# Third block of the experts' first layer by seven products of 256 tokens, with its operand sums moved and the schedule's table renewed

## The chip, the core and the metric

The kernel runs on one core of a Trainium2 chip. A core has five engines that run side by side, each through its own list of instructions in a fixed order: TensorE (PE) for matmuls, VectorE (DVE), ScalarE (ACT) and GpSimd (POOL) for elementwise work, and SyncE (SP), which here starts DMAs. Matmul results land in PSUM, eight banks of 128 rows by 512 floats; everything else lies in SBUF. The metric is the device time of one execution in microseconds (us): 1002.8 us before, the median of three runs (1002.5 to 1004.2).

## The reference, cut to what matters

Three stages follow one another: attention in which a query sees only keys of the same hash bucket, a gated layer, and four experts whose outputs are weighted and added.

```
bits   = (q @ proj > 0), (k @ proj > 0);  bucket = sum bits * 2**i      # 2 x 8 heads, 768 tokens, 64 wide
scores = where(bucket_q == bucket_k, scale * q @ k.T, -1e9);  attn = softmax(scores) @ v
x      = attn, heads side by side                                       # 1536 tokens x 512
x      = ((x @ w1) * (x @ w2)) @ w3 @ w_out                             # 1024 wide inside, 512 out
p      = domain_probs / (sum + 1e-9)
out    = sum over e of p[:, e] * (relu(x @ W1[e]) @ W2[e])              # 4 experts, 512 -> 1024 -> 512
```

## The kernel before

All products are made at nearly fp32 accuracy: every operand is split into a rounded part and the rest ("hi" by a copy to fp32r, `hi_of` L154 on ACT or `pool_hi` L160; "lo" by a subtraction, `lo_of` L157 on DVE or `pool_lo` L163), and a product is three matmuls, hi x hi, hi x lo and lo x hi (`T3`). A full matmul is 128 x 128 weights against 512 columns. The 1536 tokens go in three blocks of 512.

*Attention.* 48 units (`unit`, L405), each 256 queries of one head: scores into PSUM (`s_ps`), a minimum with its row value on DVE (L426), the exponential on ACT (L429), a normalisation on POOL or ACT, twelve transposes on PE, their split by ACT (L466) and DVE (L468), and twelve 256-column matmuls with v (`pv_ps`). `head` (L312) loads and splits q and k and copies pieces between tiles by DMA on SP's queue; v comes by L362 in rows of 64 floats. Beside it the first gate weights are loaded (L196) and split (`conv64`, L180), and a quarter of block 0's gate layer is multiplied as a filler.

*Gate.* Both products of the gate for all blocks, then w3 times w_out (`W`), then for each block eight steps `H` (24 half-size groups, twelve matmuls each) that multiply the gate's result, split just before by ACT and DVE into one of two `hl` tiles, into four banks: `o_ps` for blocks 0 and 2, `u_ps` for block 1.

*Experts.* An expert's hidden layer goes in four quarters of 256 columns. Blocks 0 and 1 are multiplied together by seven products M1 to M7 in place of eight (a Strassen scheme in Winograd's form: sums of quadrants of x on one side, of W1 on the other), six full matmuls each, in the order 4, 3, 1, 2, 5, 7, 6. ACT copies M4 and M3 out of PSUM; DVE adds the others to running sums (`mix`, L933 with L881): two sums from each of M1, M2 and M5, one from M7 and M6. A bank of the four `u_ps` comes free when its last reader is done. Block 2's part of the quarter follows as two plain groups `U` (L974) of twelve full matmuls, and then `put_down` multiplies block 0's part of the quarter by W2 (24 full matmuls). After four quarters come blocks 1 and 2 against W2.

The operand sums of x for M1, M3, M4, M6 and M7 are made once, in the third block's H steps: L859 on POOL, ten of 128 x 512, each followed by a hi on ACT and a lo on DVE into `xh` and `slot` tiles. W1 is split by POOL (`conv_full`, L730, whole tile: L161 then L164), and its five sums per quarter by DVE (L750) with a hi on ACT (L155) and a lo on DVE into `slotl` and `zs`.

*What sets the order.* The program lists operations with an engine, an assumed duration, what they need, and a priority; `emit_all` (L244) plays them once through at build time and so fixes every engine's order. The priority of attention's operations is shifted by the table `RANK` (L25); operations of the later stages take their place from a running clock.

## Time and profile before

| | us |
|---|---|
| three runs, median | 1002.8 (1002.5 to 1004.2) |
| the profiled execution | 1005.64 |
| its span on the core | 1003.9 |
| PE busy, DVE busy, ACT busy, POOL busy | 977.6, 662.0, 432.4, 313.4 |
| attention, until PE is in the gate's late part | about 274 |

The profile was taken in one execution of 1005.64 us; about 1.7 us of it lie around the span. TensorE had its full clock (the granted clock is 1.00 in every stretch). Matmuls overlap one another, so PE's busy share says little about how full it is; how many matmuls began in a stretch says more. The chain of waits, followed back from the last instruction, lies on PE for 73% and on DVE for 18%.

### The profile page before, as it was taken

How to read it: one execution, taken by the hardware profiler on the slowest of the kernel's cores; microseconds unless marked ns; L12 is line 12 of the kernel's file. 1: busy time of each engine (PE TensorE's matmuls, PEld its weight loads, DVE VectorE, ACT ScalarE, POOL GpSimd, SP SyncE). 2: the span in 40 equal slices, each digit the busy share in tenths (PEclk: the TensorE clock that was granted, in tenths of full speed). 3: DMA queues.
4: the chain of work that ended last, by engine and by line, in shares of the span. 5: the costliest groups of instructions: out<-in, count | busy, mean ns of one | idle time of the engine just before them, and what ended most of it. 6: DMA issues, size and time to landing. Idle time of an engine off the chain costs nothing.

```text
span 1003.9 us, 13346 instructions
## 1 busy us (share of the span) xinstructions
PE 977.6 (97%) x4939; PEld 822.7 (82%) x4939; DVE 662.0 (66%) x1194; ACT 432.4 (43%) x779; POOL 313.4 (31%) x297
## 2 busy tenths in 40 slices
PE   7899999999999999999799999999999999999998
PEld 6788888988788888888588888888888888888886
DVE  6799999998499984954965444554445544455343
ACT  5789999988533332434422221222212222122121
POOL 6777788764000000041641204212042120421000
PEclk9999999999999999999999999999999999999999
DMA  5853554321033331320210101101011010100012
GB/s 159 192 130 79 130 122 107 93 61 42 1 105 121 124 113 39 109 84 1 63 43 26 38 1 57 49 26 39 0 59 48 27 37 1 57 28 21 1 50 77
DMA packets 51137, 64.13 MB, mean 64 GB/s; under 512 B 17688, under 2 KB 34072, under 8 KB 51072
## 3 DMA queue, kind: packets, MB, share of 16 engines
q1 hardware_dynamic: 50928, 63.27, 22.1%
q8 instruction: 39, 0.64, 0.3%
q14 instruction: 26, 0.21, 0.1%
q10 hardware_dynamic: 144, 0.01, 0.0%
HBM read 47.22 MB, written 3.15 MB: 50 GB/s over the span
## 4 chain that ended last, share of the span: by engine, by line
PE 73%; DVE 18%; ACT 3%; issue 2%; DMA 2%; POOL 1%; SPq 0%; DVEq 0%; ACTq 0%
PE u_ps L149 50%; PE o_ps L149 19%; DVE et L468 5%; DVE e L426 5%; PE t_ps L149 2%; DMA r<-in_qk 1%; ACT e L429 1%; DVE xa L487 1%; PE pv_ps L149 1%; PE t_ps L460 1%; PE s_ps L149 1%; ACT et L466 1%; DVE hl L158 1%; DVE xh L158 1%; DVE hl L876 1%
## 5 line engine op out<-in xcount | busy, mean ns | idle before, releaser
L149 PE MATMUL u_ps<-xh,slot 128*128 128x512 f32 x768 | 179.9, 389 | 1.2 <-DVE xh L158 1.2
L149 PE MATMUL o_ps<-slotl,hl 128*128 128x512 f32 x768 | 178.2, 390 | 0.4 <-DVE hl L876 0.2
L149 PEld LDWEIGHTS u_ps<-xh,slot 128*128 128x128 f32 x768 | 144.1, 188 | 31.5 <-DVE xh L158 1.6
L149 PEld LDWEIGHTS o_ps<-slotl,hl 128*128 128x128 f32 x768 | 143.9, 188 | 31.5 <-DVE hl L876 1.7
L881 DVE TENSOR_TENSOR m<-m,u_ps 128x512 f32<-128x512 f32 x96 | 62.9, 683 | 138.4 <-ACT m L155 114.7
L161 POOL TENSOR_SCALAR slot<-wraw 128x1024 fp32r<-128x1024 f32 x16 | 17.3, 1080 | 384.6 <-DVE slotl L158 184.1
L149 PE MATMUL u_ps<-xh,slotl 128*128 128x512 f32 x480 | 111.6, 389 | 0.0
L149 PEld LDWEIGHTS u_ps<-xh,slotl 128*128 128x128 f32 x480 | 90.1, 188 | 18.7
L468 DVE TENSOR_TENSOR et<-t_ps,et 128x512 fp32r<-128x512 f32 x144 | 96.5, 680 | 5.3 <-ACT et L466 4.7
L429 ACT ACTIVATE e<-e,sm 128x768 f32<-128x768 f32 x96 | 89.6, 934 | 12.3 <-DVE e L426 10.8
L426 DVE TENSOR_SCALAR_CACHE_REDUCE e<-s_ps 128x768 f32<-128x768 f32 x96 | 90.3, 945 | 4.3 <-PE t_ps L460 3.1
L149 PE MATMUL pv_ps<-et,vv 128*128 128x256 f32 x576 | 91.8, 295 | 0.9 <-DVE xa L487 0.7
L460 PE MATMUL t_ps<-ident,e 128*128 128x128 f32 x576 | 85.6, 276 | 6.7 <-DVE et L468 4.8
L466 ACT ACTIVATE et<-t_ps 128x512 fp32r<-128x512 f32 x144 | 83.0, 593 | 12.5 <-PE t_ps L460 5.8
L149 PE MATMUL u_ps<-slotl,hl 128*128 128x512 f32 x384 | 87.7, 389 | 0.0
L149 PEld LDWEIGHTS u_ps<-slotl,hl 128*128 128x128 f32 x384 | 72.1, 188 | 15.0
L460 PEld LDWEIGHTS t_ps<-ident,e 128*128 128x128 f32 x576 | 65.2, 140 | 16.9 <-DVE et L468 7.9
L149 PEld LDWEIGHTS pv_ps<-et,vv 128*128 128x128 f32 x576 | 75.0, 190 | 3.4 <-DVE xa L487 2.8
L439 POOL TENSOR_SCALAR e<-e,sm 128x768 f32<-128x768 f32 x72 | 65.7, 921 | 18.4 <-DVE sm L444 15.0
L155 ACT ACTIVATE m<-u_ps 128x512 f32<-128x512 f32 x32 | 19.1, 598 | 107.0 <-PE u_ps L149 107.0
L873 ACT ACTIVATE hl<-m 128x512 fp32r<-128x512 f32 x32 | 20.3, 633 | 92.3 <-DVE m L881 92.3
L876 DVE SCALAR_TENSOR_TENSOR hl<-gl,hl 128x512 fp32r<-128x512 f32 x32 | 23.8, 742 | 54.3 <-ACT hl L995 46.2
(142 smaller groups left out, 1534.9 us busy)
## 6 DMA issues: line engine op xcount, KB each, us to landing
wraw<-in_e SPq DMA_DIRECT2D x64, 256.0 KB
wraw<-in_w SPq DMA_DIRECT2D x16, 512.0 KB
wraw<-in_w3T SPq DMA_DIRECT2D x16, 512.0 KB
r<-in_qk SPq DMA_DIRECT2D x15, 384.0 KB
wraw<-in_w_out SPq DMA_DIRECT2D x8, 512.0 KB
rv<-in_v SPq DMA_DIRECT2D x16, 192.0 KB
out<-xa SPq DMA_DIRECT2D x12, 256.0 KB
ka<-hh SPq DMA_DIRECT2D x15, 192.0 KB
```

What stands on the lines that cost most here:

```text
L149: nc.tensor.matmul(out=o, lhsT=l, rhs=r, start=start, stop=stop)
L155: nc.scalar.activation(out=dst, in_=ps, func=AF.Copy)
L158: nc.vector.tensor_tensor(out=dst, in0=ps, in1=f(hi), op=ALU.subtract)
L426: op(("mx", u, t), "DVE", 873, lambda ps=ps, m=m, e=e: nc.vector.tensor_scalar(out=e, in0=ps[:, 0:S], scalar1=THR, scalar2=None, op0=ALU.m ...
L429: op(("ex", u, t), "ACT", 921, lambda e=e, m=m, rs=rs: nc.scalar.activation(out=e, in_=e, func=AF.Exp, scale=-1.0, bias=m, accum_out=rs), ...
L439: return "POOL", 872, lambda: nc.gpsimd.tensor_scalar(out=e, in0=e, scalar1=r[:, t:t + 1], scalar2=1.0, op0=ALU.mult, op1=ALU.mult)
L460: nc.tensor.transpose(out=ps[:, k, t * 128:(t + 1) * 128], in_=e_t[2 * (u % ER) + t][:, kt * 128:(kt + 1) * 128], identity=ident)
L466: op(("hi", n), "ACT", 480, lambda ps=ps, et=et: nc.scalar.activation(out=et[:, 0], in_=ps, func=AF.Copy), [("T", u, j), ("pv", n - NET)], Tj)
L468: op(("lo", n), "DVE", 602, lambda ps=ps, et=et: nc.vector.tensor_tensor(out=et[:, 1], in0=ps, in1=f(et[:, 0]), op=ALU.subtract), [("hi", ...
L873: op(key, "ACT", 480, lambda: nc.scalar.activation(out=hl_t[n % 2][:, 0], in_=m_t[m], func=AF.Relu), after, clock[0])
L876: op(key, "DVE", 602, lambda: nc.vector.scalar_tensor_tensor(out=hl_t[n % 2][:, 1], in0=src(), scalar=0.0, in1=f(hl_t[n % 2][:, 0]), op0=A ...
L881: nc.vector.tensor_tensor(out=out, in0=a, in1=b, op=o)
```

## The change

*Products.* Block 2 no longer has the plain groups `U`. Its 512 tokens are taken as two halves of 256, and seven products N1 to N7 (same scheme, same W1 sums, order 4, 3, 1, 2, 5, 7, 6) of six matmuls of 256 columns each stand in their place; the results are joined by `mix` on 256 columns straight into the tiles that are kept. `mul` and `mix` get a width and an operand set. The W1 tile itself is now needed only in two of its four pieces, and POOL splits these two alone, in four instructions of 128 x 256. The W1 sums of the next quarter may overwrite the old ones once the N products, not the M products, have read them.

*Operands.* Block 2's result is copied out of `o_ps` (ACT), five sums of halves are made on DVE (`ys`), and seven operands are split (`yi` on ACT, `yd` on DVE). The sums for the M products move from POOL to DVE, one source in PSUM; M4's are made one block earlier.

*Loads and the first head.* v lies in memory so that a row of 1.5 KB per partition holds a head. The first head's query bits are written in two pieces (256 and 512 columns), and the next head's lo part is queued behind them on DVE. The load of head 2 waits for more of head 0's operations. The assumed durations and the table are new, so that attention's order is another on every engine.

```diff
 RANK = {
...
-    "ex0": -95.56,
-    "ex1": -444.49,
+    "ex0": 16.57,
+    "ex1": -26.35,
...
-            op(("ld", hh), "SP", 1130, lambda: load(slice(0, 2 * D)), [("l", hh - RR)] if hh >= RR else [],
+            op(("ld", hh), "SP", 2000, lambda: load(slice(0, 2 * D)), [(x, hh - RR) for x in (("l", "k1", "k2", "k3", "dq") if hh == RR else ("l",))],
                -1e9 + 1e7 * hh if first else T - 8000)
             if first:
...
-                op(("l", hh), "DVE", 870, lambda: scaled_lo(nc.vector), [("h", hh)], T, g)
+                op(("l", hh), "DVE", 1000, lambda: scaled_lo(nc.vector), [("h", hh), ("mq", 0)], T, g)
...
-        op(("lv", hh), "SP", 600, lambda: nc.sync.dma_start(out=rv, in_=v[b, h].rearrange("(k p) d -> p k d", p=128)),
+        op(("lv", hh), "SP", 1000, lambda: nc.sync.dma_start(out=rv, in_=v[b, h].rearrange("p (k d) -> p k d", k=NK)),
...
-        op(("mk", 0), "DVE", 865, lambda: is_pos(kb[k], ps, k), [("bm", -1)], T, "b0")
-        op(("mq", 0), "DVE", 865, lambda: is_pos(lo[64:64 + PC], ps, q), [("mk", 0)], T, "b0")
-        keys[("sf", n)] = keys[("mq", 0)]
+        op(("mk", 0), "DVE", 930, lambda: is_pos(kb[k], ps, k), [("bm", -1)], T, "b0")
+        for i, (key, c) in enumerate(((("mq", 0), slice(0, 256)), (("sf", n), slice(256, S)))):
+            op(key, "DVE", (330, 600)[i], lambda c=c: is_pos(lo[64:64 + PC, c], ps, q, c), [("mk", 0)], T + i, "b0")
...
+            rq = r.rearrange("p (j k f c) -> p j f k c", j=2, k=2, f=2)
+            for i in range(2):
+                key = ("dd" if i else "dc", name)
+                op(("dh", name, i), "POOL", 310, lambda i=i: pool_hi(a_at(fp, i)[:, 0], rq[:, i, i]), got + after, T)
+                op(key, "POOL", 640, lambda i=i: pool_lo(a_at(fp, i)[:, 1], rq[:, i, i], a_at(fp, i)[:, 0]), [("dh", name, i)], T)
...
+            for m, o, a, b in ((4, ALU.subtract, (1, 0), (0, 0)), (3, ALU.subtract, (0, 1), (1, 1)), (1, ALU.add, (0, 0), (1, 1)),
+                               (2, None, (0, 0), None), (5, None, (1, 1), None), (7, ALU.add, (1, 0), (1, 1)), (6, ALU.add, (0, 0), (0, 1))):
...
+                op(("yi", m), "ACT", 520, lambda m=m, src=src: hi_of(by(m)[:, 0], src()), ready, T + 9 * Q)
+                op(("yd", m), "DVE", 602, lambda m=m, src=src: lo_of(by(m)[:, 1], src(), by(m)[:, 0]), [("yi", m)], T + 9 * Q)
...
+        for m, a, (b, c), o in sums:
             for k in range(2):
-                op(("xs", m, k), "POOL", 1225, lambda m=m, a=a, b=b, o=o, k=k: nc.gpsimd.tensor_tensor(
-                    out=xs(m)[:, k], in0=G[a[0]][:, a[1] + k], in1=G[b[0]][:, b[1] + k], op=o),
...
+                op(("xs", m, k), "DVE", 602, lambda m=m, a=a, b=b, c=c, o=o, k=k, hb=hb: nc.vector.tensor_tensor(
+                    out=xs(m, k), in0=hb[a + k], in1=G[b][:, c + k], op=o),
...
-            for ff in (2 * fp, 2 * fp + 1):
-                n, free_ = take_u()
...
-                op(("U", e, 2, ff), "PE", 12 * 227, go, free_ + have_u + x_in + [("hl", 2, d) for d in range(KM)], clock[0])
...
+            for m, dst, lhs in ((4, C21, lambda fp=fp: a_at(fp, 1)), (3, C12, lambda fp=fp: a_at(fp, 0))):
+                n, got = mul(m, lhs, have_u, "N", by, W)
+                op(("uf", n), "ACT", 270, lambda n=n, dst=dst: hi_of(dst(), u_ps[n % 4][:, 0:256]), got + old + y_in, clock[0])
+                keys[key(f"y{m}")] = keys[("uf", n)]
+            n, got = mul(1, lambda: z(0), have_z, "N", by, W)
+            mix("ya1", C11, C21, n, ALU.add, got + old + y_in + [key("y4")], W)
+            mix("yb1", C22, C12, n, ALU.add, got + old + y_in + [key("y3"), key("ya1")], W)
```

PE in the second quarter of the first expert, from M6 (operands `slot` and `zs`) on. Before: M6, the two plain groups of block 2, and the start of the product with W2.

```order
L149 MATMUL u_ps_3041<-slot_63,zs 128x512 x6
L149 MATMUL u_ps_3038<-xh_3020,slot_65 128x512 x12
L149 MATMUL u_ps_3039<-xh_3020,slot_65 128x512 x12
L149 MATMUL o_ps_3042<-slotl_3022,hl_3029 128x512 x3
L149 MATMUL o_ps_3043<-slotl_3022,hl_3029 128x512 x3
```

The two plain groups are 24 matmuls of 512 columns.

Now, at the same place:

```order
L149 MATMUL u_ps_3040<-slot_63,zs 128x512 x6
L149 MATMUL u_ps_3041<-xh_3021,slot_64 128x256 x6
L149 MATMUL u_ps_3042<-xh_3021,slot_64 128x256 x6
L149 MATMUL u_ps_3043<-xh_3021,slotl_3022 128x256 x6
L149 MATMUL u_ps_3040<-xh_3021,slotl_3022 128x256 x6
L149 MATMUL u_ps_3041<-slot_65,slotl_3022 128x256 x6
L149 MATMUL u_ps_3042<-y,slotl_3022 128x256 x6
L149 MATMUL u_ps_3043<-slot_65,zs 128x256 x6
L149 MATMUL o_ps_3044<-slotl_3023,hl_3030 128x512 x3
```

The seven rows of 128x256 are N4, N3, N1, N2, N5, N7 and N6 in the place of the two rows of 128x512 x12; N6 now reads `zs` seven products later than M6 did.

PE in the first quarter of the first expert, behind the third block's last H step, from M6 on. Before:

```order
L149 MATMUL u_ps_3040<-slot_63,zs 128x512 x6
L149 MATMUL u_ps_3041<-xh_3020,slot_64 128x512 x12
L149 MATMUL u_ps_3038<-xh_3020,slot_64 128x512 x12
L149 MATMUL o_ps_3042<-slotl_3026,hl_3029 128x512 x3
L149 MATMUL o_ps_3043<-slotl_3026,hl_3029 128x512 x3
L149 MATMUL o_ps_3044<-slotl_3026,hl_3029 128x512 x3
```

The order is that of the other quarters.

Now, at the same place, down to N7:

```order
L149 MATMUL u_ps_3042<-slot_63,zs 128x512 x6
L149 MATMUL u_ps_3043<-xh_3021,slot_64 128x256 x6
L149 MATMUL o_ps_3044<-slotl_3027,hl_3030 128x512 x3
L149 MATMUL o_ps_3045<-slotl_3027,hl_3030 128x512 x3
L149 MATMUL o_ps_3046<-slotl_3027,hl_3030 128x512 x3
L149 MATMUL o_ps_3047<-slotl_3027,hl_3030 128x512 x3
L149 MATMUL u_ps_3043<-slot_65,slotl_3022 128x256 x6
L149 MATMUL u_ps_3042<-xh_3021,slotl_3022 128x256 x6
L149 MATMUL u_ps_3040<-xh_3021,slot_64 128x256 x6
L149 MATMUL u_ps_3041<-xh_3021,slotl_3022 128x256 x6
L149 MATMUL u_ps_3040<-y,slotl_3022 128x256 x6
```

Here the N products are taken apart: N4 alone, then half of the product with W2 (the four rows of `o_ps`), then N5, N2, N3, N1 and N7; behind the rows shown come the other half (`hl_3031`), N6 and M4 of the second quarter. `u_ps_3042` and `u_ps_3040` are the banks of M6 and M5.

DVE behind the third block's last H step. Before: the last W1 sums (`slotl`, `zs`), block 2's four lo parts out of `o_ps`, and the first mixes (`m`, `g`) of the first quarter.

```order
L158 TENSOR_TENSOR zs<-zf,zs 128x256
L158 TENSOR_TENSOR xh_3020<-o_ps_3042,xh_3020 128x512
L158 TENSOR_TENSOR xh_3020<-o_ps_3043,xh_3020 128x512
L158 TENSOR_TENSOR xh_3020<-o_ps_3044,xh_3020 128x512
L158 TENSOR_TENSOR xh_3020<-o_ps_3045,xh_3020 128x512
L881 TENSOR_TENSOR m_3034<-m_3032,u_ps_3040 128x512
L881 TENSOR_TENSOR m_3035<-m_3033,u_ps_3040 128x512
L881 TENSOR_TENSOR m_3032<-m_3032,u_ps_3041 128x512
L881 TENSOR_TENSOR m_3035<-m_3035,u_ps_3041 128x512
L881 TENSOR_TENSOR g_67<-m_3033,u_ps_3038 128x512
```

Only four lo parts (sources in PSUM) stand between the W1 sums and the first mixes.

Now: sums of halves (`gl_3028`), lo parts of the N operands (`xh_3021`, `slot_65`, `y`) and mixes in turn. First piece:

```order
L158 TENSOR_TENSOR zs<-zf,zs 128x256
L875 TENSOR_TENSOR gl_3028<-gl_3029 128x512 x2
L924 TENSOR_TENSOR m_3035<-m_3033,u_ps_3042 128x512
L158 TENSOR_TENSOR xh_3021<-gl_3028,xh_3021 128x2x256
L924 TENSOR_TENSOR m_3036<-m_3034,u_ps_3042 128x512
L924 TENSOR_TENSOR m_3033<-m_3033,u_ps_3043 128x512
L158 TENSOR_TENSOR xh_3021<-gl_3028,xh_3021 128x2x256
L924 TENSOR_TENSOR m_3036<-m_3036,u_ps_3043 128x512
L919 SCALAR_TENSOR_TENSOR hl_3030<-m_3033,hl_3030 128x512
```

The first two sums of halves and two lo parts have come ahead of mixes.

and the piece behind it:

```order
L875 TENSOR_TENSOR gl_3028<-gl_3029 128x512
L158 TENSOR_TENSOR xh_3021<-gl_3029,xh_3021 128x2x256
L158 TENSOR_TENSOR slot_65<-gl_3029,slot_65 128x512
L158 TENSOR_TENSOR xh_3021<-gl_3028,xh_3021 128x2x256
L875 TENSOR_TENSOR gl_3028<-gl_3029 128x512 x2
L158 TENSOR_TENSOR y<-gl_3028,y 128x512
L158 TENSOR_TENSOR slot_65<-gl_3028,slot_65 128x512
L924 TENSOR_TENSOR g_67<-m_3034,u_ps_3040 128x512
L924 TENSOR_TENSOR g_67<-m_3036,u_ps_3042 128x512
L924 TENSOR_TENSOR m_3035<-m_3035,u_ps_3040 128x512
```

From the first sum of halves to the last row shown, which is the last reader of M5's bank, stand 20 instructions; before there were four lo parts and then the mixes.

SP at the start of attention. Before, a load of gate weights (`wraw<-in_w`, 512 KB) stands behind the load of head 3:

```order
L324 DMA r_112<-in_qk 128x768
L196 DMA wraw_68<-in_w 128x2x512
L327 DMA ka_89<-ll_85 64x768
L327 DMA ka_86<-hh_78 64x768
L327 DMA kb_90<-hh_78 64x768
L324 DMA r_111<-in_qk 128x768
```

The next load of q and k (`r_111`) is queued behind it.

Now, further down the queue:

```order
L325 DMA r_112<-in_qk 128x768
L328 DMA ka_87<-hh_79 64x768
L328 DMA kb_91<-hh_79 64x768
L363 DMA rv_113<-in_v 128x384
L328 DMA ka_87<-ll_83 64x768
L197 DMA wraw_68<-in_w 128x2x512
L328 DMA ka_88<-hh_80 64x768
```

The load of gate weights has moved back, behind copies and a load of v.

## Rows read from the trace of the kernel before

**Rows 1.** The chain of waits over the span: start, length, engine and tile, instructions.

```profile
7.51 2.39 DVE ll L330
...
30.38 8.73 DMA r<-in_qk
...
260.58 1.43 PE pv_ps L149 x12
...
448.13 21.77 PE u_ps L149 x96
...
513.29 5.44 PE o_ps L149 x24
518.73 14.96 PE u_ps L149 x66
```

**Rows 2.** What PE waited for: engine, tile, releaser: total us, times, longest us.

```profile
PE o_ps L149 <- DVE hl L158: 5.2, 5, 1.5
...
PE s_ps L149 <- DVE ll L377: 1.4, 1, 1.4
```

**Rows 3.** Stretches: length, busy us (instructions) of PE, PEld, DVE, ACT, POOL, clock, DMA share.

```profile
25.00:50.00 25.00, 20.58 (x148) 18.54 (x147) 19.84 (x43) 19.25 (x39) 19.86 (x23) 1.00 0.85 194
...
100.00:150.00 50.00, 48.66 (x355) 44.31 (x354) 49.52 (x107) 46.73 (x93) 40.16 (x48) 1.00 0.52 125
475.00:500.00 25.00, 19.85 (x83) 14.78 (x82) 25.00 (x23) 11.41 (x20) 18.70 (x10) 1.00 0.17 49
```

**Rows 4.** Page, weight loads of attention's last product: busy us, mean ns, idle before.

```profile
L149 PEld LDWEIGHTS pv_ps<-et,vv 128*128 128x128 f32 x576 | 75.0, 190 | 3.4 <-DVE xa L487 2.8
```

**Rows 5.** Timeline of a later quarter, the W1 sums: start, length, engine, line, operation [idle before].

```profile
653.68 1.76 DVE L750 SCALAR_TENSOR_TENSOR zf<-wraw 128x256 f32<-128x256 f32 x5
...
655.22 1.06 ACT L155 ACTIVATE slotl<-zf 128x1024 fp32r<-128x1024 f32 x1 [0.73 <-DVE zf L750]
...
656.55 1.22 DVE L158 TENSOR_TENSOR slotl<-zf,slotl 128x1024 fp32r<-128x1024 f32 x1
```

**Rows 6.** Timeline of the third block's H steps, POOL and DVE.

```profile
471.08 0.69 DVE L158 TENSOR_TENSOR hl<-xa,hl 128x512 fp32r<-128x512 f32 x1 [2.51 <-ACT hl L155]
...
476.75 1.73 POOL L859 TENSOR_TENSOR cbuf<-g,gl 128x512 f32<-128x512 f32 x1
477.26 1.77 DVE L158 TENSOR_TENSOR hl<-xa,hl 128x512 fp32r<-128x512 f32 x1
```

**Rows 7.** Timeline behind the third block's last H step.

```profile
497.69 2.64 ACT L155 ACTIVATE xh<-o_ps 128x512 fp32r<-128x512 f32 x4
...
499.52 1.52 PE L149 MATMUL u_ps<-xh,slot 128*128 128x512 f32 x6
...
501.08 0.60 ACT L155 ACTIVATE m<-u_ps 128x512 f32<-128x512 f32 x1 [0.76 <-PE u_ps L149]
...
502.44 2.64 DVE L881 TENSOR_TENSOR m<-m,u_ps 128x512 f32<-128x512 f32 x4 [0.54 <-PE u_ps L149]
503.25 2.41 POOL L164 TENSOR_TENSOR slot<-wraw,slot 128x1024 fp32r<-128x1024 f32 x1
```

**Rows 8.** Timeline of the first head: PE's bits, DVE's two bit rows, POOL.

```profile
8.02 0.28 PE L149 MATMUL s_ps<-ll,pbh 128*128 128x256 f32 x1
...
9.92 1.08 DVE L377 TENSOR_SCALAR kb<-s_ps,thr,amp 12x768 fp32r<-12x768 f32 x1
...
11.03 1.07 DVE L377 TENSOR_SCALAR ll<-s_ps,thr,amp 12x768 fp32r<-12x768 f32 x1
...
14.01 0.92 POOL L351 TENSOR_SCALAR r<-r,svec 128x768 f32<-128x768 f32 x1 [2.67 <-issue]
```

**Rows 9.** DMA view of 193.5:203, one load of v alone: queue, packets, MB, share.

```profile
q1 hardware_dynamic: 784, 0.20, 9.1%
```

**Rows 10.** DMA view of 36:40, v beside gate weights.

```profile
q1 hardware_dynamic: 853, 0.49, 100.5%
```

**Rows 11.** DMA view of 50:60, q and k alone.

```profile
q1 hardware_dynamic: 178, 0.45, 21.3%
```

More of the change, by code (lines that the diff above doesn't have):

```diff
@@ L225, in tile_lsh_attention_moe @@
         "NONE": {"PE": 0, "ACT": 0, "DVE": 0, "POOL": 0, "SP": 0},
-        "SP": {"PE": 2300, "ACT": 2300, "DVE": 2300, "POOL": 2300, "SP": 2300, "NONE": 0},
+        "SP": {"PE": 1900, "ACT": 1900, "DVE": 1900, "POOL": 1900, "SP": 1900, "NONE": 0},
     }
@@ L671, in up, with hl @@
         return n
+    def hl(n):
+        return hl_t[n % (2 if n < KF * NB else 3)]
     def take_hl():
@@ L833, in tile_lsh_attention_moe @@
         if blk == NB - 1:
+            done = [("H", blk, ff) for ff in range(KF)] + [("gdone", blk, ff) for ff in range(KF)]
             for d in range(KM):
-                op(("hh", blk, d), "ACT", 480, lambda blk=blk, d=d, hb=hb: hi_of(XH[blk][:, 0, d], hb[d]),
-                   [("H", blk, KF - 1)] + after, T)
-                op(("hl", blk, d), "DVE", 602, lambda blk=blk, d=d, hb=hb: lo_of(
-                    XH[blk][:, 1, d], hb[d], XH[blk][:, 0, d]), [("hh", blk, d)], T)
-            continue
@@ L840, in tile_lsh_attention_moe, with half @@
-        for d in range(KM):
-            op(("hl", blk, d), "ACT", 480, lambda blk=blk, d=d, hb=hb: hi_of(G[blk][:, d], hb[d]),
-               [("H", blk, KF - 1)] + [("gdone", 0, ff) for ff in range(KF)], T)
-        d, m = (0, 2) if blk == 0 else (2, 5)
-        xdone = []
+                op(("hl", blk, d), "ACT", 480, lambda blk=blk, d=d, hb=hb: hi_of(G[blk][:, d], hb[d]), done, T)
+            q = [[("hl", blk, 2 * j + k) for k in range(2)] for j in range(2)]
+            def half(j, c):
+                return G[2][:, 2 * j:2 * j + 2, c * 256:(c + 1) * 256]
@@ new lines, in tile_lsh_attention_moe @@
+            for m, o, a, b in ((4, ALU.subtract, (1, 0), (0, 0)), (3, ALU.subtract, (0, 1), (1, 1)), (1, ALU.add, (0, 0), (1, 1)),
+                               (2, None, (0, 0), None), (5, None, (1, 1), None), (7, ALU.add, (1, 0), (1, 1)), (6, ALU.add, (0, 0), (0, 1))):
+                src = (lambda a=a: half(*a)) if o is None else (lambda m=m: ysum(m))
+                ready = q[0] + q[1] + after
+                if o is not None:
+                    op(("ys", m), "DVE", 602, lambda m=m, o=o, a=a, b=b: nc.vector.tensor_tensor(
+                        out=ysum(m), in0=half(*a), in1=half(*b), op=o), ready + [(x, m_, k) for x, m_ in (("xd", 5), ("xs", 3)) for k in range(2)] +
+                       ([("yd", 4)] if m == 6 else []), T + 9 * Q)
+                    ready = ready + [("ys", m)]
+                op(("yi", m), "ACT", 520, lambda m=m, src=src: hi_of(by(m)[:, 0], src()), ready, T + 9 * Q)
+                op(("yd", m), "DVE", 602, lambda m=m, src=src: lo_of(by(m)[:, 1], src(), by(m)[:, 0]), [("yi", m)], T + 9 * Q)
@@ L845, in tile_lsh_attention_moe @@
+            continue
         TX = T + 9 * Q
         def split(m, k, src, ready):
-            op(("yh", m, k), "ACT", 520, lambda: hi_of(bx(m)[:, 0, k], src()), ready, TX)
+            op(("yh", m, k), "ACT", 520, lambda: hi_of(bx(m)[:, 0, k], src()), ready + after, TX)
             op(("xd", m, k), "DVE", 602, lambda: lo_of(bx(m)[:, 1, k], src(), bx(m)[:, 0, k]), [("yh", m, k)], TX)
+        done = [("H", blk, KF - 1)] + [("gdone", 0, ff) for ff in range(KF)]
+        kept_d, first_d, m0 = ((0, 1, 2, 3), 0, 2) if blk == 0 else ((2, 3), 2, 5)
@@ new lines, in tile_lsh_attention_moe @@
+        sums = ((4, 2, (0, 0), ALU.subtract),) if blk == 0 else (
+            (3, 0, (1, 2), ALU.subtract), (1, 2, (0, 0), ALU.add), (7, 2, (0, 2), ALU.add), (6, 0, (0, 0), ALU.add))
+        readers = [[("hc", blk, d)] if d in kept_d else [] for d in range(KM)]
+        for m, a, (b, c), o in sums:
+            for k in range(2):
+                op(("xs", m, k), "DVE", 602, lambda m=m, a=a, b=b, c=c, o=o, k=k, hb=hb: nc.vector.tensor_tensor(
+                    out=xs(m, k), in0=hb[a + k], in1=G[b][:, c + k], op=o),
+                   done + [("hc", b, c + k)] + ([("xd", 4, k)] if m == 7 else []), TX)
+                readers[a + k].append(("xs", m, k))
+                split(m, k, lambda m=m, k=k: xs(m, k), [("xs", m, k), ("W", KF - 1)])
@@ L912, in tile_lsh_attention_moe @@
         order = [[] for _ in range(NB)]
-        old = x_in + [("gl", nh[0] - 1 - k) for k in range(16 if e else 0)]
+        old = x_in + y_in + [("gl", nh[0] - 1 - k) for k in range(16 if e else 0)]
         for fp in range(4):
@@ new lines, in part @@
+            def part(i, c, fp=fp):
+                return lambda: kept(2, 2 * fp + i)[:, c * 256:(c + 1) * 256]
+            C11, C12, C21, C22 = (part(i, c) for i in range(2) for c in range(2))
+            for m, dst, lhs in ((4, C21, lambda fp=fp: a_at(fp, 1)), (3, C12, lambda fp=fp: a_at(fp, 0))):
+                n, got = mul(m, lhs, have_u, "N", by, W)
+                op(("uf", n), "ACT", 270, lambda n=n, dst=dst: hi_of(dst(), u_ps[n % 4][:, 0:256]), got + old + y_in, clock[0])
+                keys[key(f"y{m}")] = keys[("uf", n)]
@@ new lines, in tile_lsh_attention_moe @@
+            mix("y12", C12, C12, n, ALU.subtract, got + [key("yb1")], W)
+            mix("ya2", C11, C11, n, ALU.add, got + [key("ya1"), key("y12")], W)
+            n, got = mul(7, lambda: z(3), have_z, "N", by, W)
+            mix("y11", C11, C11, n, ALU.add, got + [key("ya2")], W)
+            n, got = mul(6, lambda: z(4), have_z, "N", by, W)
+            mix("y22", C22, C22, n, ALU.add, got + [key("yb2")], W)
+            for k in range(2):
+                kept_key[2 * fp + k] = [key(f"y{k + 1}{c + 1}") for c in range(2)]
```

191 lines of the change are left out of this document (101 added, 90 removed).

## The prediction, made before the result

> **What bounds the kernel now.** I read the chain of waits first. From the gate on it lies on TensorE in long unbroken pieces, and two spacings can be worked out of them: 96 full matmuls in 21.77 us, 24 in 5.44 and 66 in 14.96 make 226.7 ns each, and twelve of 256 columns in attention make 1.43 us, 119.2 ns each [rows 1]. So where PE is not kept waiting, time is the number of matmuls, and half as many columns cost 0.526 of a full one. Next come PE's waits: the largest is for `hl` from DVE, 5.2 us in five waits, all under `o_ps` [rows 2]; that is the third block's H steps. Third, the stretches. From 25 to 50 us PE, DVE and ACT are all a fifth or more idle with the DMA engines busy 0.85; from 100 to 150 DVE works 49.52 of 50 us, so attention's steady part is DVE's; and from 475 to 500 DVE is busy for the whole 25.00 us with 23 instructions, over a microsecond each, while PE begins only 83 matmuls [rows 3].
>
> Three places are touched: the quarters of the experts (PE bound), the third block's H steps and the quarter behind them (DVE bound), and the start of attention (loads and the first head).
>
> **The quarters.** Per quarter 24 full matmuls go, 24 x 0.2267 = 5.44 us, and 42 of 256 columns come, 42 x 0.1192 = 5.01 us: 0.435 us less, in 15 later quarters 6.5 us. The 256-column price is that of `pv_ps`, where a weight load lasts 190 ns on its own and yet the spacing stays at 119 [rows 1, 4]; the new products have the same shape, other tiles. What could take the gain back: the W1 sums for the next quarter must now wait for N6 instead of M6. Five sums, their hi and their lo take from 653.68 to 657.77, 4.1 us, but only hi and lo, 1.06 and 1.22 us [rows 5], need the old ones gone; behind N6 stand 5.44 us of W2 and M4 and M3 (2.72 us) before the next M1 needs them, so 8.2 us cover about 3. The banks: N3 needs M5's bank, whose second reader on DVE ends about 4.9 us behind M1's end at 0.66 us a mix (2.64 for four [rows 7]); PE wants it 6.2 us behind it. N2, N1 and N6 come out with 0.9 to 1.3 us to spare in the same way. I take 6.5; if these margins went, DVE's extra mixes would cost up to 1 us in each quarter, 15 us.
>
> Here the Trainium skill speaks against the change. Its page "TensorE: Matmul & The Clock Gate", section "Back-to-back issue gap", gives a sustained spacing of about 81 ns for 128 columns and 131 ns for 512, so that half the columns cost well over half the time: between the two, 256 columns would be an estimated 98 ns, 0.75 of a full matmul. By that rule a quarter would lose some 1.7 us and the kernel some 26; the trace disagrees on both sizes (226.7 and 119.2 ns), and the measurement decides.
>
> **The third block's H steps.** They and the first quarter take from 469.90 (448.13 + 21.77) to 513.29, 43.39 us [rows 1], for 96 matmuls of H, 42 of M and 24 of U: 162 x 0.2267 = 36.72. So PE stood for 6.67 us here. The reason is in the timeline: a lo of `hl` on DVE, both sources in SBUF, lasts 0.69 us alone, but 1.77 beside POOL's operand sum of 1.73 [rows 6], and PE waits for just these. The change takes ten such sums from POOL to DVE, where one source lies in PSUM; mixes with a PSUM source keep 0.66 us even beside POOL's 2.41 us conversion [rows 7]. DVE gets eight of them here, 8 x 0.66 = 5.3 us more in a stretch of 27 us (M4's two fall a block earlier), and its some 26 SBUF instructions shrink from up to 1.77 to 0.69. Left beside them are POOL's W1 conversions, which stretch about four lo's; I put the stall at 2 us, with 0 (all hidden) and 6.7 (as before) as ends. Gain 4.7.
>
> The Trainium skill, "SBUF — State Buffer", section "Who interferes with whom", has the same as a rule: a DVE instruction with two SBUF inputs contends with a GpSimd instruction that reads SBUF, one with at most one SBUF input does not, and the loser is fully blocked. The trace agrees (1.77 against 0.69 us, and 0.66 from PSUM). By full blocking a 2.41 us conversion could cost a lo 2.4 us, and the stall left would be an estimated 4.8 us rather than 2.
>
> **The first quarter behind them.** Here DVE has most to do. Set T0 at M3's start, 499.52 before. The third block's four copies out of `o_ps` end about 0.8 us behind it, M3's copy 2.2 behind, and the first mix starts 2.9 behind, when M1 is done [rows 7]; that holds afterwards too. In the new order 18 instructions follow from that mix to the last reader of M5's bank (`m_3035<-m_3035,u_ps_3040`): at 0.65 us that is T0 + 14.6. M6 ends at 8.2, N4 at 8.9 (its bank and operand come at 7.0), half of W2's product at 11.6, N5 at 12.3. Now PE stands: N2 needs M6's bank at 14.1 and N3 M5's at 14.8, so N3, N1 and N7 end at about 17.2, the rest of W2 at 19.9 and N6 at 20.6, against 18.6 without a wait. That is 2.0 us. I add 0.3 for DVE waiting on ACT's hi parts of the last two operands, and 1 us for contention, since 11 of these 18 have both sources in SBUF and POOL splits W1 beside them (ends 0 and 3). Then comes the wait that is new: in this quarter nothing of W2 is left behind N6, so only M4 and M3, 2.72 us, stand before M1. ACT's hi of the W1 sums is queued behind the copy of M4; M4 ends 1.36 behind N6, its copy 0.9 later (M3's ended 2.2 behind its start [rows 7]), then 1.06 + 1.22 us [rows 5] and a launch: M1 is 2.0 us late. Queued behind that hi on ACT is M3's copy, with which nobody is late before M1. Sum of new stalls 5.3 us. With this quarter's own 0.43 us of fewer matmuls the stretch changes by 2 + 5.3 - 6.67 - 0.43 = +0.2 us; its ends are -7.1 (no stall at all) and +7 (H as before, all contention).
>
> **The start of attention.** The first head's key bits wait on DVE for the second lo (7.51 to 9.90 [rows 1]) though PE had the bits done by 8.3; now that lo is behind them. The query bits, 1.07 us for 768 columns [rows 8], are cut to the 256 that the first scores need. This could bring the first scores forward by 1.6 + 0.7 us; other loads and copies also end there, so I take 1. POOL runs the scaling of head 3 (0.92 us [rows 8]) ahead of the first normalisation; now behind it: 0.9. Two loads of gate weights wait longer on SP's queue, and v comes in a sixth of the descriptors (128 rows for 768). The chain has 8.73 us of waiting for q and k from 30.38 [rows 1]. A load of v alone costs 9.1% of 9.5 us, 0.87 us of all DMA engines [rows 9]; beside gate weights the two fill 4.0 us [rows 10], of which the weights' 0.3 MB need 1.4 at the rate of q and k (0.45 MB in 2.13 us [rows 11]). So v costs up to 1.7 us more there, and three loads of v fall before 45 us: 0 to 5.2, I take 2. Together 4 us, ends 0 and 8.4. It lasts to the end, since DVE has no idle time later in attention to lose it in [rows 3].
>
> That same fullness is the danger: the table changes every engine's order in all 48 units. What the order shows moved I could not price for each unit, so I cost it at nothing, hidden as now behind DVE, with both signs open: 0.1 us a unit is 5 us.
>
> **Sum.** -6.5 + 0.2 - 4 = -10.3 us on the profiled 1005.64 (span 1003.9 and 1.7 around it): 995.3. That execution stands 2.8 us above the median of the runs, 1002.8; taken from the median, 992.5.
>
> **The rivals.** (A) the forecast: 988 to 997. (B) The stretch from the H steps to the second quarter loses its stalls: if DVE finds time, the region gives 7 us more, about 986; for it speaks that DVE gives up all its stretched instructions, against it the 18 in a row. (C) The start gives nothing, since q and k of later heads set the pace whatever waits: 996.5; with the H steps stalled as before too, 1001. For it speaks the 8.73 us piece for q and k, against it that crowding is part of this piece. (D) Slower: attention's new order puts an instruction with a wait ahead of the DVE work that paces it. DVE has 0.5 us idle in 50 now [rows 3], so each added wait is paid in full; 0.3 us in each of 48 units is 14.4 us, and the time 1007. It decides from 10.3 / 48 = 0.21 us a unit. Against it: a new order need not wait more than the old. (E) A 256-column matmul of the new kind is held to its weight load: 190 ns [rows 4] make 42 x 0.19 - 5.44 = +2.54 us a quarter, 16 quarters +41, and with the rest unchanged 1040. Speaking against it: 576 such matmuls of attention at 119 ns. The rule of the Trainium skill quoted above ("Back-to-back issue gap") would end in this rival, with 0.75 of a full matmul instead of 0.84.
>
> **How the numbers follow.** A 0.50, B 0.14, C 0.22, D 0.11, E 0.03. Two us, 0.2%, is what can be told from no change here. A and B are faster; C is faster in 0.18 of its 0.22 and within 0.2% in 0.04; D holds 0.02 within 0.2%, 0.09 slower, E all slower. Faster 0.82, the same 0.06, slower 0.12. The range leaves out half of D, E and the far end of B: 985 to 1002.
>
> **What would show it.** Quarters from the second on 19.97 us long instead of 20.40; twelve 256-column matmuls of N in 1.43 us; waits of PE for `hl` from DVE under 3 us in all; PE waits of some 2 us each ahead of N2 or N3 in the first quarter and ahead of the second quarter's M1; the gate's last fill starting about 4 us earlier. The forecast is wrong if attention ends later than 274 us, if quarters stay at 20.4, or if PE waits in each quarter for a bank.

## The result, and the profile after

The changed kernel takes 994.77 us (median of four runs, 993.28 to 996.28), the kernel before 1003.06 on the same chip: a ratio of 0.9916, 95% interval 0.9898 to 0.9934, so 8.4 us less (6.6 to 10.2). The forecast was 10.3 us less, 992.5 with a range of 985 to 1002. The two profiled executions stand further apart than the medians, 12.4 us in the span (1003.9 and 991.5), since that of before was longer than its timed runs and that of after is the lowest of its four; the steps are measured between these two traces. Where in the trace of before its extra microseconds lie is not known.

The chain of waits of the changed kernel (start, length, engine and tile, instructions) answers to [rows 1]:

```profile
263.91 125.22 PE u_ps L149 x551
...
439.38 21.17 PE u_ps L149 x93
...
526.63 5.47 PE o_ps L149 x24
532.10 14.55 PE u_ps L149 x84
546.65 5.47 PE o_ps L149 x24
552.12 14.55 PE u_ps L149 x84
```

PE's long piece in the gate, which began at 273.97 before, begins at 263.91: the start, up to the end of attention, gives 10.1 us. From 532.10 to 552.12 a quarter takes 20.02 us, where before it took 14.96 + 5.44 = 20.40.

The other borders of the stages are read from PE's timeline: the first H step of the third block (`o_ps`) and the second quarter's M2, first before,

```profile
469.73 8.55 PE L149 MATMUL o_ps<-hl,slotl 128*128 128x512 f32 x37
...
522.64 2.88 PE L149 MATMUL u_ps<-xh,slotl 128*128 128x512 f32 x12
```

then after, with the first quarter's M3 (before, M3 starts at 499.52 [rows 7]):

```profile
461.05 3.11 PE L149 MATMUL o_ps<-hl,slotl 128*128 128x512 f32 x13
...
489.00 1.52 PE L149 MATMUL u_ps<-xh,slot 128*128 128x512 f32 x6
...
515.99 2.89 PE L149 MATMUL u_ps<-xh,slotl 128*128 128x512 f32 x12
```

| stage, us | before | after | after less before |
|---|---|---|---|
| start to PE's long piece in the gate | 273.97 | 263.91 | -10.1 |
| from there to the third block's H steps | 195.8 | 197.1 | +1.4 |
| H steps, to M3 of the first quarter | 29.8 | 28.0 | -1.8 |
| from M3 to M2 of the second quarter | 23.1 | 27.0 | +3.9 |
| from there to the end of the span | 481.3 | 475.5 | -5.8 |

Most of the 1.4 us in the second row are lost where PE, late in the gate, waits 0.69 us for a split on ACT and then takes 3.32 us for twelve matmuls where other such twelves take 2.88:

```profile
436.05 3.32 PE L149 MATMUL o_ps<-hl,slotl 128*128 128x512 f32 x12 [0.69 <-ACT slotl L155]
```

e1 below, with the experts of before, has the same wait, and e2, with the attention of before, has not, so it came with the new order of attention; in which way, no run follows.

The stretches of the changed kernel (length, busy us and instructions of PE, weight loads, DVE, ACT, POOL, then clock, DMA share, GB/s) answer to [rows 3]:

```profile
25.00:50.00 25.00, 25.00 (x188) 23.56 (x186) 23.36 (x51) 23.23 (x48) 22.68 (x29) 1.00 0.69 195
...
100.00:150.00 50.00, 48.57 (x354) 44.74 (x355) 49.42 (x107) 46.00 (x91) 39.72 (x48) 1.00 0.43 107
```

From 25 to 50 us PE begins 188 matmuls in place of 148 and is busy throughout, with the DMA engines at 0.69 instead of 0.85. From 100 to 150 hardly anything differs. Most of attention's gain is made in the first 75 us: by then PE is 61 matmuls ahead (482 against 421), which at the 7.1 a microsecond of the later stretches is 8.6 us.

Around the H steps (timelines of DVE, POOL and PE; in square brackets the idle time before and what ended it), to lay beside [rows 6]:

```profile
467.23 4.16 DVE L158 TENSOR_TENSOR slot<-m,slot 128x512 fp32r<-128x512 f32 x2
...
476.72 2.81 DVE L158 TENSOR_TENSOR hl<-gl,hl 128x512 fp32r<-128x512 f32 x1
...
489.83 3.60 DVE L875 TENSOR_TENSOR gl<-gl 128x512 f32<-128x512 f32 x2 [4.25 <-ACT gl L155]
```

```profile
468.15 2.69 POOL L164 TENSOR_TENSOR slotl<-wraw,slotl 128x1024 fp32r<-128x1024 f32 x1
...
476.59 2.39 POOL L164 TENSOR_TENSOR slotl<-wraw,slotl 128x1024 fp32r<-128x1024 f32 x1
...
490.18 2.72 POOL L164 TENSOR_TENSOR slotl<-wraw,slotl 128x1024 fp32r<-128x1024 f32 x1
```

```profile
472.65 5.73 PE L149 MATMUL o_ps<-hl,slotl 128*128 128x512 f32 x24 [2.56 <-DVE hl L158]
479.58 5.51 PE L149 MATMUL o_ps<-hl,slotl 128*128 128x512 f32 x23 [1.20 <-DVE hl L158]
...
502.28 0.98 PE L149 MATMUL u_ps<-slot,slotl 128*128 128x256 f32 x6 [1.36 <-ACT gl L155]
503.93 0.98 PE L149 MATMUL u_ps<-xh,slotl 128*128 128x256 f32 x6 [0.67 <-DVE g L924]
...
509.76 0.88 PE L149 MATMUL u_ps<-slot,zs 128*128 128x256 f32 x6
...
513.70 0.73 PE L149 MATMUL u_ps<-slot,slotl 128*128 128x512 f32 x2 [0.32 <-ACT slotl L155]
514.96 1.20 PE L149 MATMUL u_ps<-slot,slotl 128*128 128x512 f32 x4 [0.53 <-DVE slotl L158]
```

What PE waits for, over the whole span, answers to [rows 2]:

```profile
PE o_ps L149 <- DVE hl L158: 4.0, 3, 2.6
```

Each long DVE instruction has a POOL instruction with two inputs (L164) beside it: two lo's take 4.16 us next to one of 2.69, a single one 2.81 next to 2.39, two sums of halves 3.60 next to 2.72. PE waits 2.56 and 1.20 us for `hl` behind the first two, and its waits for `hl` make 4.0 us in all, where the forecast wanted under 3. Further down stand the waits of the first quarter: 1.36 ahead of N5, 0.67 ahead of N2, and at 513.70 and 514.96 M1 of the second quarter, with waits of 0.32 and 0.53 for the hi and the lo of the W1 sums, which have a queue ahead of them (below, e8).

### The profile page after: what moved, and what is told of

Read it like the earlier page. It is cut to its first block, busy times and chain, and to the rows that moved or that the text cites. A ratio compares the mean times of both kernels' runs of the same rounds, so it can differ in the third digit from the quotient of the medians.

```text
span 991.5 us, 14182 instructions
## 1 busy us (share of the span) xinstructions
PE 970.0 (98%) x5227; PEld 832.6 (84%) x5227; DVE 718.1 (72%) x1341; ACT 428.6 (43%) x784; POOL 280.9 (28%) x319
## 4 chain that ended last, share of the span: by engine, by line
PE 81%; DVE 12%; ACT 4%; issue 2%; POOL 0%; DVEq 0%; ACTq 0%; POOLq 0%
PE u_ps L149 49%; PE o_ps L149 19%; PE s_ps L149 5%; PE pv_ps L149 3%; PE t_ps L462 3%; DVE et L470 3%; DVE e L428 2%; PE t_ps L149 1%; ACT e L431 1%; ACT et L468 1%; DVE hl L919 1%; DVE xa L489 1%; PE t_ps L517 1%; DVE slot L158 1%; DVE hl L158 1%
## 5 line engine op out<-in xcount | busy, mean ns | idle before, releaser
L149 PE MATMUL u_ps<-xh,slotl 128*128 128x512 f32 (+1 forms) x672 | 137.5, 359 | 0.7 <-DVE g L924 0.7
L149 PEld LDWEIGHTS u_ps<-xh,slotl 128*128 128x128 f32 x672 | 114.3, 189 | 19.6 <-DVE g L924 0.9
L161 POOL TENSOR_SCALAR slot<-wraw 128x256 fp32r<-128x256 f32 x32 | 14.9, 468 | 404.8 <-DMA wraw<-in_e 224.4
L149 PE MATMUL u_ps<-xh,slot 128*128 128x512 f32 (+1 forms) x576 | 116.1, 354 | 1.2 <-DVE xh L158 1.2
L149 PEld LDWEIGHTS u_ps<-xh,slot 128*128 128x128 f32 x576 | 97.1, 189 | 18.0 <-DVE xh L158 1.6
L149 PE MATMUL pv_ps<-et,vv 128*128 128x256 f32 x576 | 89.1, 292 | 0.7 <-DVE xa L489 0.4
L441 POOL TENSOR_SCALAR e<-e,sm 128x768 f32<-128x768 f32 x72 | 68.5, 960 | 16.9 <-DVE sm L446 15.7
L161 POOL TENSOR_SCALAR slotl<-wraw 128x1024 fp32r<-128x1024 f32 x16 | 17.0, 1062 | 156.6 <-PE o_ps L149 125.2
```

The costliest lines, as they stand in the source:

```text
L149: nc.tensor.matmul(out=o, lhsT=l, rhs=r, start=start, stop=stop)
L161: nc.gpsimd.tensor_scalar(out=o, in0=i, scalar1=1.0, scalar2=1.0, op0=ALU.mult, op1=ALU.mult)
L441: return "POOL", 872, lambda: nc.gpsimd.tensor_scalar(out=e, in0=e, scalar1=r[:, t:t + 1], scalar2=1.0, op0=ALU.mult, op1=ALU.mult)
```

## The experiments

Every run has its own comparison with the kernel before on its chip, so ratios are compared, and stage times are read from each run's trace. "Gate" is the start of PE's piece of 125.2 us.

| run | us | ratio to before (95%) | gate | H steps to M3 | M3 to M2 of the next quarter |
|---|---|---|---|---|---|
| before | 1003.06 | 1 | 273.97 | 29.8 | 23.1 |
| changed | 994.77 | 0.9916 (0.9898 to 0.9934) | 263.91 | 28.0 | 27.0 |
| e1 | 997.32 | 0.9920 (0.9903 to 0.9936) | 264.01 | | |
| e2 | 1002.62 | 0.9968 (0.9955 to 0.9981) | 273.13 | | |
| e3 | 994.06 | 0.9889 (0.9875 to 0.9904) | 264.26 | | |
| e4 | 1006.39 | 1.0016 (1.0006 to 1.0026) | 277.05 | | |
| e5 | 1010.04 | 1.0062 (1.0047 to 1.0077) | 279.25 | | |
| e6 | 1021.15 | 1.0172 (1.0155 to 1.0189) | 290.37 | | |
| e7 | 991.53 | 0.9880 (0.9865 to 0.9894) | 263.82 | 25.4 | 28.3 |
| e8 | 993.34 | 0.9898 (0.9883 to 0.9913) | 264.77 | 28.0 | 25.6 |
| e9 | 996.61 | 0.9913 (0.9886 to 0.9941) | 265.25 | | |
| e10 | 995.88 | 0.9914 (0.9894 to 0.9934) | 265.50 | | |
| e11 | 1012.43 | 1.0079 (1.0059 to 1.0100) | 284.35 | | |
| e12 | 989.85 | 0.9855 (0.9834 to 0.9876) | 265.69 | 25.4 | 25.4 |

**e1 and e2: the two halves of the change.** e1 takes attention (everything ahead of the gate's late part, v's layout with it) from the changed kernel and the rest from before; e2 the other way round.

> Attention of the changed kernel (table, durations, v rows, first head), gate and experts of the kernel before. Theory, by the two profiles: PE's long piece in the gate starts at 263.9 instead of 274.0 us, so about 10 us are the start of attention, and this half alone gives 993 to 995 us. Rival (the experts' half brings the gain, attention's end is a shift that the gate's wait for weights takes back): over 999 us.

> Attention of the kernel before, gate, H steps and experts of the changed kernel. Theory: fifteen quarters give 5.9 us, the third block with the first quarter takes 2.9 back, so 3 us less than before: 999 to 1001 us. Rival (the stretch behind the third block loses nothing, as forecast): 996.5 us. Rival (a lower granted clock with the new products eats the gain): 1002 us or more, with a clock under 0.997.

e1 is 8 us faster than before and its gate starts at 264.01; e2 is 3.2 us faster with its gate at 273.13. Attention is most of the gain, and the experts' half brings little: its quarters give, its first quarter takes. In absolute time both came out higher than expected (993 to 995 and 999 to 1001), but on their chip the kernel before takes 1005.03. e2's median of 1002.62, with a median clock of 0.996, meets the numbers of its last rival, that a lower clock eats the gain. It does not bear that rival out, since the gain by ratio is the 3 us of the theory; the kernel before has a median clock of 0.998 there, so that a small cost of the clock stays open. The two ratios multiply to 0.989, some 3 us below the whole change's 0.9916 and at the edge of what the intervals allow.

**e3: v in rows of 256 bytes again.**

```diff
-  v[b, h].rearrange("p (k d) -> p k d", k=NK)
+  v[b, h].rearrange("(k p) d -> p k d", p=128)
...                                              # and v in memory as it was before
```

> The changed kernel with v loaded in rows of 64 floats again (768 rows instead of 128 per head); every instruction and its order stays. Theory of the forecast: short rows cost up to 1.7 us a load where transfers crowd, some 2 us in all: about 2 us slower than the changed kernel. Rival (transfers are hidden or the loads come at other times): no difference, under 0.5 us. Rival (the row length is most of the start's 10 us): 6 us or more slower.

The gate starts 0.35 us later than in the changed kernel, and the time is not longer. So the long rows are worth nothing that can be seen here, though the first 50 us then hold 3832 packets under 512 bytes. The term of 2 us falls.

**e4 and e11: table and assumed durations.** e4 is the changed kernel with both from before; e11 has the new table with the old durations.

```diff
 RANK = {            # e4: old values; e11: new values
-  op(("ld", hh), "SP", 2000, ...)      # and the other assumed durations of attention
+  op(("ld", hh), "SP", 1130, ...)
```

> The changed kernel with the table and the assumed durations of attention from the kernel before; v rows, first head and the wait of head 2's load stay as changed. Theory: the order of loads and splits that the table sets is most of the start's gain: PE's long piece in the gate starts at 269 to 273 us and the time is 5 to 9 us over the changed kernel. Rival (v rows and the first head's edits carry it): the piece starts at 264 to 267 us, at most 3 us over the changed kernel.

> The changed kernel with the assumed durations and latencies of attention from the kernel before and the new table. If the table alone carries the start's gain: PE's long piece in the gate starts at 263 to 267 us and the time is within 3 us of the changed kernel. If the table fits only the durations it was made for: it starts at 269 us or later.

With both old the gate starts at 277.05, beyond the 269 to 273 of the theory and 3 us later than before although v's rows and the first head's edits are in; with the new table on the old durations at 284.35. So the table alone does not bring the gain, and neither do the other edits alone. That a table is good only for the durations that it was made with fits both runs; the old table with the new durations was not run.

**e5, e6 and e9: the gate weights' loads.** The change moves the first two 512 KB loads from 26.3 and 39.1 to 42.7 and 46.7 us, and before these a piece of 8.73 us in the chain is a wait for q and k [rows 1]. e5 moves them back in the kernel before, e6 forward in the changed one, both by what the planner (the pass at build time that fixes every order) is told, so that it makes new orders; e9 moves only the two entries of SP's queue.

```diff
-  CR = (3, 2)                                      # e5, in the kernel before
+  CR = (7, 2)
...
-  ... t - (1.5 * P if key == "cl" else 0))         # e6, end of a line
+  ... t - (1e9 if key == "cl" and n < 2 and T is None else 1.5 * P if key == "cl" else 0))
...
+  for k, x in (("cl", 0), ("ld", 5)), (("cl", 1), ("lv", 2)):     # e9, on the finished order
+      order.remove(keys[k]); order.insert(order.index(keys[x]) + 1, keys[k])
```

> The kernel before with one change: the first loads of gate weights may start from the seventh unit on instead of the third, so they leave SP's queue among the loads of heads 3 to 6. Theory (the 512 KB loads, at 26.3 and 39.1 us before and at 42.7 and 46.7 in the changed kernel, are what delays q and k by the 8.73 us piece, and with it the start): PE's long piece in the gate starts 4 to 9 us earlier than 274.0. Rival (the table's order on DVE, ACT and POOL is the gain): under 2 us earlier, or later since the conversion of the weights is crowded behind.

> The changed kernel with one change: the first two loads of gate weights go out as soon as the third unit's exponential allows (before head 4's loads), as in the kernel before. Theory: they delay q and k again, PE's long piece in the gate starts 4 to 9 us later than 263.9. Rival: under 2 us later.

> The changed kernel with two entries of SP's queue moved and every other engine's order unchanged: the first load of gate weights directly behind head 5's load of q and k, the second behind head 2's load of v, as they stood in the kernel before. Theory (these 1 MB among the loads of heads 5 to 7 make q and k late): PE's long piece in the gate starts 4 to 9 us later than 263.9. Rival (the transfers fit, and the gain was in the order on the other engines): under 1 us later.

e5 went against the theory: its gate starts 5.3 us later than before, not 4 to 9 earlier. e6 went the way of the theory and far beyond it, 26.5 us for the 4 to 9 expected. e5's stretches:

```profile
25.00:50.00 25.00, 24.80 (x182) 22.67 (x181) 22.67 (x48) 22.21 (x46) 20.53 (x24) 1.00 0.68 178
...
100.00:150.00 50.00, 45.09 (x320) 40.01 (x319) 48.15 (x101) 44.41 (x90) 39.47 (x46) 1.00 0.45 112
```

From 25 to 50 us it begins 182 matmuls, nearly as many as the changed kernel, so with the loads out of the way the early stall is gone; from 100 to 150 it begins 320 instead of 355. The new order that came with the edit costs more than the stall that went. e6 is a new order too (317 from 100 to 150), so neither run tells the loads from the order. e9 leaves every other queue as it is, and there the theory falls. Its loads, as they are issued:

```profile
23.87 0.33 SPq L325 DMA_DIRECT2D r<-in_qk  x1
24.25 0.45 SPq L197 DMA_DIRECT2D wraw<-in_w  x1
...
29.16 0.34 SPq L325 DMA_DIRECT2D r<-in_qk  x1
...
33.41 0.42 SPq L197 DMA_DIRECT2D wraw<-in_w  x1
...
36.74 0.34 SPq L325 DMA_DIRECT2D r<-in_qk  x1
```

```profile
25.00:50.00 25.00, 25.00 (x188) 23.55 (x186) 23.34 (x51) 23.23 (x48) 22.79 (x29) 1.00 0.75 197
...
100.00:150.00 50.00, 47.57 (x346) 43.68 (x347) 49.04 (x104) 46.34 (x93) 38.94 (x47) 1.00 0.41 104
```

The weights' loads go out at 24.25 and 33.41, yet from 25 to 50 us PE begins the same 188 matmuls as in the changed kernel. The gate's 1.3 us come from 100 to 150 (346 for 354), where e12, with the changed kernel's order in attention, has 349 and a gate at 265.69; the gates of this one order lie between 263.82 (e7) and 265.69, so the 1.3 us are within what it does from run to run.

What the loads did in the kernel before is seen at the heads of its queues (timelines of ACT, POOL and PE, with the idle time before):

```profile
32.79 0.68 ACT L198 ACTIVATE cbuf<-wraw 128x512 f32<-128x512 f32 x1 [1.47 <-DMA wraw<-in_w]
33.37 1.57 ACT L466 ACTIVATE et<-t_ps 128x512 fp32r<-128x512 f32 x3
```

```profile
39.19 0.91 POOL L351 TENSOR_SCALAR r<-r,svec 128x768 f32<-128x768 f32 x1 [2.33 <-DMA kb<-bt]
```

```profile
35.62 1.16 PE L460 MATMUL t_ps<-ident,e 128*128 128x128 f32 x8 [1.52 <-DVE et L468]
...
40.54 0.59 PE L149 MATMUL s_ps<-ka,hh 128*128 128x512 f32 x2 [2.80 <-issue]
```

ACT stands 1.47 us for the landing of `wraw`, because the conversion (L198) is queued ahead of the splits of `et`, and PE stands 1.52 for these. POOL stands 2.33 us for the transfer of the bits, and PE 2.80; for the latter the profile names no releaser, but the matmul behind it reads `ka` and `hh`, which DMAs fill. In the changed kernel the conversion comes to ACT at 49.67 us, and PE has no wait over 0.91 us between 10 and 62. So a late transfer cost what stood behind it in a queue. This fits e5 and e9, but no run on the order of before moves these loads alone, so it is read and not shown.

**e10: the first head's lo.**

```diff
+  order.remove(keys["l", 1]); order.insert(order.index(keys["mk", 0]), keys["l", 1])
```

> The changed kernel with one instruction of DVE moved: head 1's lo stands ahead of the first head's bits again, all other orders unchanged. Theory of the forecast: the first scores come 1 to 1.6 us later, and since DVE is full later in attention PE's long piece in the gate starts 1 to 2 us later. Rival (other loads and copies end at the same time anyway): under 0.5 us.

The gate starts at 265.50, 1.6 us later than in the profile of the changed kernel, but between those of e8 (264.77) and e12 (265.69), which share its attention order. All three were profiled at a mean clock of 0.93 in the first 25 us, the changed kernel at 1.00. So the gate does not tell the effect apart. The place itself does: the first minimum over scores on DVE starts 0.3 us later than in the changed kernel (0.5 later than in e8 and e12), where the theory said 1.0 to 1.6. First the changed kernel, then e10:

```profile
11.33 0.95 DVE L428 TENSOR_SCALAR_CACHE_REDUCE e<-s_ps 128x768 f32<-128x768 f32 x1
```

```profile
11.63 0.96 DVE L428 TENSOR_SCALAR_CACHE_REDUCE e<-s_ps 128x768 f32<-128x768 f32 x1
```

**e7, e8 and e12: the stretch behind the third block.** e7 makes the lo of three W2 tiles on DVE; e8 puts the hi of the W1 sums ahead of M4's copy on ACT; e12 has both.

```diff
...
+  if name[0] == "O" and name[1] == 0 and name[2] > 0:                       # e7; otherwise as before, on POOL
+      op(("dd", name), "DVE", 1220, lambda: lo_of(slots[dst][:, 1], r, slots[dst][:, 0]), [("dh", name)], T)
...
-  ... got + prev + [("xd", 3, k) for k in range(2)], clock[0])              # e8, M4's and M3's copy, end of a line
+  ... got + prev + [("xd", 3, k) for k in range(2)] + ([("zh", name, 1)] if (e, fp) == (0, 1) else []), clock[0])
```

> The changed kernel with the lo parts of the first expert's last three W2 tiles made on DVE (1.22 us each) instead of POOL (2.4 to 2.7 us each); PE's order is the same. Theory (a DVE instruction with both sources in SBUF stands still for POOL's whole two-input conversion): the DVE instructions of 4.16 (two), 2.81 and 3.60 us (two) fall to 1.3, 0.69 and 1.3, PE's wait of 2.56 us behind them goes to under 1.3, and the stretch from the H steps to the second quarter gets 2 to 5 us shorter. Rival (they are long because they wait for ACT or for PE): they stay long and the stretch gets 2 to 4 us longer by DVE's three new instructions.

> The changed kernel with one swap on ACT: in the second quarter of the first expert the hi of the W1 sums stands ahead of M4's copy instead of behind it. Theory: M1 of that quarter waits for these sums because of this queue, so it starts 1.0 to 1.6 us earlier (513.70 and 514.96 in the changed kernel), and nothing else moves. Rival (the sums are late on DVE anyway, or the bank that M4's copy frees is then what PE waits for): less than 0.5 us.

> The changed kernel with both edits tried one by one: lo of three W2 tiles on DVE, and the hi of the W1 sums ahead of M4's copy. If they add: the second quarter's M1 starts about 3 us earlier in its stretch than in the changed kernel and the time is 990 to 991.5 us. If they overlap: 991.5 to 993.

In e7 the same DVE instructions, without POOL's two-input work beside them (DVE, then PE):

```profile
467.11 2.00 DVE L158 TENSOR_TENSOR slot<-m,slot 128x512 fp32r<-128x512 f32 x2
...
469.64 1.21 DVE L158 TENSOR_TENSOR slotl<-wraw,slotl 128x1024 fp32r<-128x1024 f32 x1
...
478.34 0.69 DVE L158 TENSOR_TENSOR hl<-gl,hl 128x512 fp32r<-128x512 f32 x1
```

```profile
471.51 10.95 PE L149 MATMUL o_ps<-hl,slotl 128*128 128x512 f32 x47 [1.50 <-DVE hl L158]
```

Two lo's fall from 4.16 to 2.00 us, the single one from 2.81 to 0.69; PE's waits of 2.56 and 1.20 become one of 1.50, and the H steps get 2.5 us shorter although DVE has two instructions of 1.2 us more there. POOL's two-input work is the cause of most of the length. The 0.7 us by which the two lo's miss the 1.3 of the theory stand beside a one-input instruction of POOL (L161, 1.05 us from 466.93). DVE is not always the one that loses: the next L161 takes 3.01 us while DVE makes lo's beside it.

```profile
474.15 3.01 POOL L161 TENSOR_SCALAR slotl<-wraw 128x1024 fp32r<-128x1024 f32 x1 [6.18 <-PE o_ps L149]
```

The next stretch got 1.3 us longer. The 24 N matmuls from N2 on take 3.24 us in the changed kernel and 4.63 in e7, first and second of these pieces of the chains:

```profile
503.93 3.24 PE u_ps L149 x24
```

```profile
501.09 4.63 PE u_ps L149 x24
```

The granted clock is 0.50 from 502 to 504 in e7. In e12, with the same edit, they take 3.23 us, so this belongs to the run.

In e8 the W1 sums and M1 (ACT, then PE):

```profile
511.42 1.06 ACT L155 ACTIVATE slotl<-zf 128x1024 fp32r<-128x1024 f32 x1 [4.40 <-PE u_ps L149]
...
513.00 0.60 ACT L155 ACTIVATE m<-u_ps 128x512 f32<-128x512 f32 x1 [0.21 <-PE u_ps L149]
```

```profile
511.35 2.91 PE L149 MATMUL u_ps<-xh,slot 128*128 128x512 f32 x12
514.10 1.52 PE L149 MATMUL u_ps<-slot,slotl 128*128 128x512 f32 x6
```

M1 follows M3 without a wait, and the stretch is 25.6 instead of 27.0 us. The time of e8 alone does not show it, since its interval overlaps that of the changed kernel. e12 shows that the two add: 50.8 us from the H steps to M2 where the changed kernel takes 54.9, 4.1 us less for 2.5 and 1.4, and 989.85 us, ratio 0.9855. It is faster than both kernels.

## Why the prediction came out as it did

*Spacing and quarters: right.* Matmuls of 256 columns cost half: 42 of them and 42 full ones take 14.55 us, which leaves 5.03 for the 42, 119.8 ns each against 119.2 forecast. A quarter gained 0.38 instead of 0.435 us; some 0.03 of the difference is that W2's 24 matmuls now take 5.47 instead of 5.44. The rest of the span lost 5.8 us where 6.5 was expected. No bank and no W1 sum was waited for in the later quarters, as forecast, and with 119.8 ns rival E is out. The sustained spacings that the Trainium skill gives, "TensorE: Matmul & The Clock Gate", section "Back-to-back issue gap", are about 131 ns for 512 columns and 81 for 128. They do not hold for this kernel, with 226.7 ns for full matmuls and 119.8 for those of 256 columns.

*The H steps: mechanism right, its size wrong.* The forecast left 2 us of the 6.7 us stall; 4.8 stayed (27.95 less 102 matmuls of 226.7 ns), a gain of 1.8 where 4.7 was forecast. The step that failed is the term of 2 us for POOL's W1 conversions, "which stretch about four lo's": no row stood behind that size, and the conversions L164 of 2.4 to 2.7 us hold a lo for nearly their whole length, 2.1 us for the single one. The other end was on record: the Trainium skill, "SBUF — State Buffer", section "Who interferes with whom", says that the loser is fully blocked, and by it 4.8 us were estimated. The trace and e7 side with it: 2.81 beside 2.39, and 0.69 without.

*The first quarter: mechanism right, stalls a little too large.* Counted from M3, N2 was put at 14.1 us and started at 14.9; N6 at 19.9 and started at 20.8; the next M1 2.0 us late, and by e8 it was 1.4. New stalls were put at 5.3 us; the stretch grew by 3.9 us, and with the 0.4 that a quarter saves the stalls measure 4.3. One wait was missed, N5's 1.36 us: N4's bank is freed by a copy on ACT that stands behind two hi's, which wait for DVE. It probably cost little, since DVE was late for N2 anyway. With the H steps the region came to +2.0 us against +0.2, and rival B, a region without stalls, is out.

*The start: the sign right, the size and the reasons wrong.* Four us were forecast and 10.1 came, 8.7 after the 1.4 lost again in the gate; rival C, no gain, is out. The terms: v's rows 2 us, measured none (e3); the first head 1 us, of which the moved lo is 0.3 to 0.5 at its place (e10) and the cut of the query bits was not tried alone; head 3's scaling on POOL 0.9, not tried alone. The step that failed is the new order "at nothing": without the new table and its durations the gate starts 13 us later (e4), so they carry most of the gain. Which of the moved operations earn it stays open. The DMA rows [rows 9 to 11] were read as a price of short rows, which e3 denies; the timelines read rather as places in queues, which is not shown. Rival D did not come, but its size was not too large: e5, e6 and e11 are other orders of attention, and their gates start 5 to 26 us late.

*The sum* of -10.3 was made of -6.5, +0.2 and -4; measured between the traces it is -5.8, +2.0, -10.1 and +1.4 (the gate), which is -12.4 by the unrounded times, and -8.4 by the timed runs. The total came out near by luck, since a start that gave far more than its term met a region and a gate that gave less: it does not vouch for its terms.
